# A fused attention and mixture-of-experts kernel: the first expert's row numbers by one-hot products, its second layer and the second expert's tiles as scheduled steps

## The chip, the cores and the metric

The kernel runs on one core of a Trainium2 chip. The metric is the time of one execution on the device in microseconds (us), lower is better. Before the change three runs gave 637.39, 641.42 and 641.85; the median is 641.42. The engines are TensorE (PE in the profile; PEld is its weight load), VectorE (DVE), ScalarE (ACT), GpSimd (POOL) and SyncE (SP), which issues most transfers. Each engine takes its instructions in the order of the program.

## The reference

```python
# q, k, v: (4, 8, 576, 64); first the sum of two attentions
out_d  = softmax(q_d @ k_d.T / 8) @ v_d          # q_d, k_d, v_d: means over 4 neighbouring positions
scores = where(|i - j| < 4, q @ k.T / 8, -1e9)   # local attention at full length
x      = repeat(out_d, 4) + softmax(scores) @ v  # then 2304 rows of 512
# then a mixture of 8 experts, two for each row
lg     = x @ w_gate + log1p(exp(x @ w_noise)) * noise
top2, wts = the two largest of lg, and their softmax
out[rows of e] += wts[:, None] * (relu(x[rows of e] @ w1[e]) @ w2[e])   # w1: 512x1024, w2: 1024x512
```

## The kernel before

**Stages.** The attention output is made in 18 chunks of 128 rows. Of each chunk TensorE makes a transposed copy that is stored as rows of x_d in memory (`l_xt`, line 690), and the router's numbers (`l_lg`, line 707, and their sum `l_ls`, line 716). Chunks are routed in groups: chunks 0 to 3, 4 to 7, 8 to 11, 12 and 13, 14 to 17. Routing a group gives noisy logits, the two best experts, each row's position in its expert's list (sums over rows as products with a triangle, `r_pos`, lines 768 to 771), and two weights. For each chunk two indirect transfers of GpSimd then scatter row number and weight into list_d in memory (`r_put`, line 836): 36 scatters in all.

**Expert 0** has 630 rows, 5 tiles of 126, made in two parts so that it can begin before the last group is routed. Part one is 3 tiles, the rows of the first three groups (`GA` = 2 is the last of them). Its row numbers come back from list_d: once the first 24 scatters are out, SyncE reads the list (`a_list`, 997), VectorE clears the empty places (`a_rows`, 1008), GpSimd gathers the rows of x (`gather0`, 1011), VectorE reorders them (`b_order`, 1106), TensorE transposes them (`b_pe`, 1113), and ScalarE and VectorE cut each tile into a high and a low half (`b_hi`, `b_lo`). Part two, 2 tiles, has its row numbers without memory: for each of the last six chunks VectorE marks, in a 128x256 table, which place of the list a row takes (`r_hot`, 787), and 12 products of these tables with the row numbers give the list (`b_list`, 800). The first layer (`b_gemm`, 1133) goes over 8 chunks of 128 hidden columns; each product with a weight is three products of halves (high by high, high by low, low by high), so 96 products for each part. The second layer (`gemm2`, 1230) is 24 products of 512 columns for each tile; VectorE scales the result (1236), and GpSimd scatters it into the output (1240).

**Experts 1 to 7** are a loop written out by hand. In the second layer of expert e the table `BESIDE` (for e = 0 the table `FIRST`) says after which product block the rows of expert e + 1 are gathered (G), turned in blocks of 32 by VectorE (`turn_xt`, 1169), moved to their places by ScalarE and VectorE (`move_xt`, 1180 and 1182) and cut in halves (H).

**What sets the order.** All up to expert 0's first layer, with the loads of its second layer's weights, is a list of `Step`s: an engine, an assumed duration, what it comes after, and a priority. `run_steps` takes for each engine the step that can begin first and among several the lowest priority, and so writes each engine's order. A table `OFF` adds a number for each kind of step to its priority. Buffers are rings; a step that needs a slot comes after the users of the slot's last owner. Where the planned clock leaves TensorE idle, `keep_warm` fills the gap with products on a tile of ones (line 373); nobody reads them. The order is fixed when the program is built; on the chip each engine waits wherever something is late.

## Time and profile before

| | before |
|---|---|
| median of three runs | 641.42 us |
| lowest, highest | 637.39, 641.85 us |
| the profiled execution, its span and its own time | 644.8 us |
| TensorE busy | 613.5 us, 95% |
| VectorE, ScalarE, GpSimd busy | 412.1, 348.7, 241.6 us |

The profiled execution is one execution recorded by the hardware profiler, 3.4 us above the median. Times in the rows are microseconds from the start of its span. The names in a row (out<-in) are those of the program's tiles: xT is a chunk of attention output, lg and m are the router's logits and choices, xr a tile of gathered rows, ptg its transpose, ph0a and ph0b the first layer of parts one and two, hot a table of marks. "x16" at a row's end counts instructions taken together. A figure in square brackets is the idle time before, with what ended it. The clock column is the share of TensorE's full clock that was granted. Matmul records overlap, since a product's tail runs beside the next product's start.

### The profile page before, as it was taken

The page shows a single profiled execution, that of the slowest core. Times are in us where ns is not written, and L with a number is a line of the kernel's source. Part 1 is how long each engine was busy: PE and PEld are TensorE (multiplying, and loading weights), DVE is VectorE, ACT ScalarE, POOL GpSimd, SP SyncE. Part 2 cuts the span into 40 slices and gives each one's busy share as a digit, 9 for nine tenths or more (in the row PEclk, how much of TensorE's full clock was granted, in tenths as well). Part 3 has the DMA queues.
Part 4 walks back from the last instruction along what each step waited for, and adds up shares of the span by engine and source line. Part 5 has one row for each costly group of instructions (what it writes and reads, how often), then busy time and mean ns, then how long its engine had stood idle before and what let it go on. Part 6 is the DMA issues. An engine that isn't in the chain of part 4 may idle for free. (4 is left out here: it accounts for less than half of the span.)

```text
span 644.8 us, 12872 instructions
## 1 busy us (share of the span) xinstructions
PE 613.5 (95%) x4770; PEld 535.4 (83%) x4770; DVE 412.1 (64%) x1029; ACT 348.7 (54%) x810; POOL 241.6 (37%) x310
## 2 busy tenths in 40 slices
PE   8989998899899999999999999999999999999993
PEld 7768686777798889988987998998899899889982
DVE  5898689688584693874676487467647736753310
ACT  7877487585543573762574376256438616733200
POOL 5574758665444223232322323323132333222111
PEclk9999899899799999999999999999999999999997
DMA  9998985776744344543654454354455436444111
GB/s 157 190 193 188 191 198 142 209 205 163 209 80 109 96 154 144 149 129 116 179 156 142 129 156 134 115 172 145 140 144 147 146 118 167 134 141 125 56 45 34
DMA packets 136760, 92.63 MB, mean 144 GB/s; under 512 B 72028, under 2 KB 118620, under 8 KB 136688
## 3 DMA queue, kind: packets, MB, share of 16 engines
q1 hardware_dynamic: 125136, 62.71, 39.6%
q0 software_dynamic: 11552, 29.01, 15.1%
q8 instruction: 39, 0.64, 0.4%
q14 instruction: 33, 0.27, 0.2%
HBM read 72.62 MB, written 19.95 MB: 144 GB/s over the span
## 5 line engine op out<-in xcount | busy, mean ns | idle before, releaser
L1205 PE MATMUL ph<-xh,w0l 128*128 128x316 f32 x448 | 138.1, 308 | 0.0
L1205 PE MATMUL ph<-xl,w0h 128*128 128x316 f32 x448 | 138.0, 308 | 0.0
L1205 PE MATMUL ph<-xh,w0h 128*128 128x316 f32 x448 | 138.0, 308 | 0.0
L1230 PE MATMUL py<-w1l,hh 128*126 128x512 f32 x320 | 126.2, 394 | 0.0
L1230 PE MATMUL py<-w1h,hh 128*126 128x512 f32 x320 | 126.2, 394 | 0.0
L1230 PE MATMUL py<-w1h,hl 128*126 128x512 f32 x320 | 126.1, 394 | 0.0
L1209 ACT ACTIVATE hh<-ph 128x632 fp32r<-128x632 f32 x56 | 39.1, 699 | 134.9 <-PE ph L1205 134.9
L1240 POOL DMA_INDIRECT out_dram<-ga,lt x40 | 45.0, 1124 | 175.2 <-DVE ga L1239 123.8
L1210 DVE SCALAR_TENSOR_TENSOR hl<-ph,hh 128x632 fp32r<-128x632 f32 x56 | 45.8, 817 | 85.5 <-ACT hh L1209 84.7
L1180 ACT ACTIVATE xr<-tr 32x128 f32<-32x128 f32 x280 | 86.3, 308 | 5.0 <-DVE tr L1169 1.1
L1205 PEld LDWEIGHTS ph<-xl,w0h 128*128 128x128 f32 x448 | 84.3, 188 | 0.3
L1205 PEld LDWEIGHTS ph<-xh,w0h 128*128 128x128 f32 x448 | 84.2, 188 | 0.3
L1205 PEld LDWEIGHTS ph<-xh,w0l 128*128 128x128 f32 x448 | 84.2, 188 | 0.0
L1230 PEld LDWEIGHTS py<-w1l,hh 128*126 128x126 f32 x320 | 59.7, 186 | 14.6
L1230 PEld LDWEIGHTS py<-w1h,hl 128*126 128x126 f32 x320 | 59.6, 186 | 14.4
L1230 PEld LDWEIGHTS py<-w1h,hh 128*126 128x126 f32 x320 | 59.6, 186 | 14.3
L1239 DVE SCALAR_TENSOR_TENSOR ga<-py,lt,ga 126x512 f32<-126x512 f32 x35 | 26.3, 751 | 68.2 <-PE py L1230 68.2
L1218 POOL DMA_INDIRECT ga<-out_dram,cl x35 | 38.1, 1090 | 83.5 <-PE ph L1205 60.9
L1182 DVE COPY xr<-tr 32x128 f32<-32x128 f32 x280 | 64.2, 229 | 3.5
L201 ACT ACTIVATE w0h<-raw 128x512 fp32r<-128x512 f32 x64 | 39.0, 624 | 37.0 <-DMA raw<-in_moe_w_dram 36.9
L1085 POOL DMA_INDIRECT gx<-x_d,cl x35 | 36.5, 1043 | 55.0 <-PE ph L1205 32.5
L836 POOL DMA_INDIRECT list_d<-pay,sli x36 | 36.8, 1022 | 34.3 <-PE pb L800 8.1
(176 smaller groups left out, 1022.8 us busy)
## 6 DMA issues: line engine op xcount, KB each, us to landing
raw<-in_moe_w_dram SPq DMA_DIRECT2D x128, 256.0 KB
vw<-in_v_dram SPq DMA_DIRECT2D x80, 64.0 KB
x_d<-x SPq DMA_DIRECT2D x18, 256.0 KB
out_dram<-zero SPq DMA_DIRECT2D x6, 768.0 KB
nat<-in_q_dram SPq DMA_DIRECT2D x16, 256.0 KB
nat<-in_k_dram SPq DMA_DIRECT2D x16, 256.0 KB
vg<-in_v_dram SPq DMA_DIRECT2D x8, 320.0 KB
vg<-in_v_dram SPq DMA_DIRECT2D x8, 256.0 KB
```

The source lines that it names most:

```text
L201: nc.scalar.activation(hi, raw, AF.Copy)
L836: ins = nc.gpsimd.indirect_dma_start(out=list_d[:, :], out_offset=bass.IndirectOffsetOnAxis(ap=sli[:, kk, i : i + 1], axis=0), in_=pay[:, ...
L1085: ins = nc.gpsimd.indirect_dma_start(out=gx, out_offset=None, in_=x_rows[:, :], in_offset=bass.IndirectOffsetOnAxis(ap=lists[e][1][:, t : ...
L1180: nc.scalar.activation(dst, src, AF.Copy)
L1182: nc.vector.tensor_copy(dst, src)
L1205: last_mm[0] = nc.tensor.matmul(ph[:, n, 0:NH], lhsT=w[:, c, :], rhs=xx[:, c, sl], start=(c == 0 and z == 0), stop=(c == NDC - 1 and z == 2))
L1209: nc.scalar.activation(hh, ph[:, :, 0:NH], AF.Relu)
L1210: nc.vector.scalar_tensor_tensor(out=hl, in0=ph[:, :, 0:NH], scalar=0.0, in1=hh.bitcast(F32), op0=ALU.max, op1=ALU.subtract)
L1218: after_pe(nc.gpsimd.indirect_dma_start(out=acc[:TR], out_offset=None, in_=out[:, :], in_offset=bass.IndirectOffsetOnAxis(ap=cl[:TR, t : t ...
L1230: last_mm[0] = nc.tensor.matmul(py[:TR], lhsT=hx[:, sl], rhs=w, start=(f == 0 and z == 0), stop=(f == NFC - 1 and z == 2))
L1239: nc.vector.scalar_tensor_tensor(out=acc[:TR], in0=py[:TR], scalar=wt, in1=acc[:TR], op0=ALU.mult, op1=ALU.add)
L1240: nc.gpsimd.indirect_dma_start(out=out[:, :], out_offset=bass.IndirectOffsetOnAxis(ap=lt[:TR, t, 0:1], axis=0), in_=acc[:TR], in_offset=No ...
```

## The change

1. *Part one's row numbers.* The first three groups get marks too: for each chunk a table of 128x256 for tiles 0 and 1 and one of half the width for tile 2 (`r_hot`, 24 marks more). For each of these groups 12 products on TensorE (`a_part`) add up to lists, and VectorE adds them over the groups (`a_acc`). The gather of part one comes after the last of these sums, no more after the list in memory. The list is still read, for the weights of part one and for what other chunks put into part two (`a_list`, `a_rows`).
2. *Second layer of expert 0* as steps: four blocks of 6 products for each tile (`o_part`), a scaling (`o_mul`) and a scatter (`o_put`), so tiles of part one can go ahead of part two's first layer.
3. *Expert 1's tiles* as steps, by the way of expert 0: reorder (`e_order`), four transposes on TensorE (`e_pe`), two halves (`e_hi`, `e_lo`), in place of turn and move. Its first-layer weights are steps too (`fetch_e`, `hi_e`, `lo_e`). The table `FIRST` goes, and the written-out loop begins at expert 1.
4. *New priorities* for nearly every kind of step, attention among them.

```diff
@@ -320,21 +320,23 @@
-        "a_count": -34.4, "a_holes": 34.1, "a_list": -12.6, "a_rows": 8.5, "b_gather": -16, "b_gemm": 8,
-        "b_rest": 24.4, "b_rows": -40, "b_weights": 40, "c_count": -49, "c_fills": -30.5, "c_first": 25.6,
...
+        "a_acc": -44.2, "a_count": -60, "a_holes": 6, "a_list": 10.6, "a_part": -60, "a_rows": 25.3,
+        "b_gather": -60, "b_gemm": 30.3, "b_hi": 10.9, "b_list": -11.9, "b_lo": -21.5, "b_order": -10.6,
+        "b_pe": -23.8, "b_relu": -27.6, "b_rest": -44.4, "b_rows": 35.1, "b_weights": -26.1, "c_count": -49,
...
@@ -782,11 +784,42 @@
                                        in1=st["pos", g][:, :ni, 0], op0=ALU.mult, op1=ALU.add)
+        def one(name):
+            return sm.tile([P, 2 * P], BF16, tag="hot", name=name, bufs=sum(ni_ for _, ni_ in groups[GA + 1 :]))
+
+        def mark_(dst, i, base):
+            nc.vector.tensor_scalar(dst, iota_b[:, : dst.shape[1]], far[:, i : i + 1], float(FAR - base), op0=ALU.subtract, op1=ALU.is_equal)
+
         for i in range(ni):
-            hot = sm.tile([P, 2 * P], BF16, tag="hot", name=f"hot{g}_{i}", bufs=sum(ni_ for _, ni_ in groups[GA + 1 :]))
-            nc.vector.tensor_scalar(hot, iota_b, far[:, i : i + 1], float(FAR - NA), op0=ALU.subtract, op1=ALU.is_equal)
-            hots.append((hot, n0 + i))
-
+            hot = one(f"hot{g}_{i}")
+            mark_(hot, i, NA if g > GA else 0)
+            if g > GA:
+                hots.append((hot, n0 + i))
+                continue
+            if i % 2 == 0:
+                two = one(f"hot{g}_{i}s")
+            rest = two[:, P * (i % 2) : P * (i % 2) + P]
+            mark_(rest, i, 2 * TR)
+            hots_a.append(((hot[:, 0:P], hot[:, TR : TR + P], rest), n0 + i))
+
+    def a_part(g):
+        pa = bank(RA, 2 * NTA, f"pa{g}").rearrange("p (t c) -> p t c", c=2)
+        for t in range(NTA):
+            for i, (hot, n) in enumerate(hots_a):
+                nc.tensor.matmul(pa[:, t], lhsT=hot[t], rhs=idp[:, n], start=(i == 0), stop=(i == len(hots_a) - 1))
+        hots_a.clear()
+        st["pa", g] = pa
+
+    def a_acc(g):
+        pa = st.pop(("pa", g))
+        if g == 0:
+            nc.vector.tensor_copy(sum_a, pa)
+        else:
+            nc.vector.tensor_tensor(sum_a, sum_a, pa, op=ALU.add)
+        if g == GA:
+            nc.vector.scalar_tensor_tensor(out=cl0[:, :NTA], in0=sum_a[:, :, 0], scalar=64.0, in1=sum_a[:, :, 1], op0=ALU.mult, op1=ALU.add)
+
+    hots_a = []
     hots = []
@@ -974,6 +1007,7 @@
     cle = xo.tile([P, NT - NTA], F32, tag="cle", name="cle")
+    sum_a = xo.tile([P, NTA, 2], F32, tag="sum_a", name="sum_a")
     scatters_by = {}
@@ -994,7 +1028,7 @@
         src = list_d[t0 * TR : t1 * TR, :]
-        ins = nc.sync.dma_start(out=lt[:TR], in_=src.rearrange("(t p) c -> p t c" if t0 else "(p t) c -> p t c", p=TR))
+        ins = nc.sync.dma_start(out=lt[:TR], in_=src.rearrange("(t p) c -> p t c", p=TR))
         wait_for(ins, scatters)
@@ -1003,9 +1037,8 @@
-        for lt, cl in ((lt0[:, :NTA], cl0[:, :NTA]), (lte, cle)):
-            ids_ = lt[:TR, :, 0]
-            nc.vector.scalar_tensor_tensor(out=cl[:TR], in0=ids_, scalar=float(N), in1=ids_, op0=ALU.is_lt, op1=ALU.mult)
+        ids_ = lte[:TR, :, 0]
+        nc.vector.scalar_tensor_tensor(out=cle[:TR], in0=ids_, scalar=float(N), in1=ids_, op0=ALU.is_lt, op1=ALU.mult)
@@ -1028,7 +1061,11 @@
         b3 = Step("r_where", "dve", 0.11, lambda g=g, n0=n0, ni=ni: r_where(g, n0, ni), after=[b3, s_holes], use=[ppb], **pr_)
-        s_hot = Step("r_hot", "dve", 0.2 + 0.2 * ni, lambda g=g, n0=n0, ni=ni: r_hot(g, n0, ni), after=[b3], light=True, prio=n1 + KH) if g > GA else None
+        s_hot = Step("r_hot", "dve", 0.2 + (0.2 if g > GA else 0.34) * ni, lambda g=g, n0=n0, ni=ni: r_hot(g, n0, ni), after=[b3, s_ids], light=True, prio=n1 + KH)
+        if g <= GA:
+            pab = buf(RA)
+            s_acc = Step("a_part", "pe", 0.07 * ni * NTA, lambda g=g: a_part(g), after=[s_hot], new=[pab], prio=n1 + KH)
+            s_acc = Step("a_acc", "dve", 0.1 if g < GA else 0.25, lambda g=g: a_acc(g), after=[s_acc], use=[pab], prio=n1 + KH)
         b5 = Step("r_slot", "dve", 0.75, lambda g=g, n0=n0, ni=ni: r_slot(g, n0, ni), after=[b3], **pr_)
@@ -1041,8 +1078,8 @@
             s_list = a1 = Step("a_list", "sp", 0.9, a_list, after=list(s_put), light=True, prio=n1 + 2.0, move=0.3)
-            a1 = Step("a_rows", "dve", 0.15, a_rows, after=[a1, s_ids], light=True, prio=n1 + 2.0)
-            s_gxa = [Step("b_gather", "pool", 1.05, lambda t=t, r=(n0 + ni) * P: b_gather(t, r), after=[a1] + s_store[: n0 + ni], light=True, prio=n1 + 2.0, lag=3.2, stage=2)
+            s_rows = Step("a_rows", "dve", 0.15, a_rows, after=[a1, s_ids], light=True, prio=n1 + 2.0)
+            s_gxa = [Step("b_gather", "pool", 1.05, lambda t=t, r=(n0 + ni) * P: b_gather(t, r), after=[s_acc] + s_store[: n0 + ni], light=True, prio=n1 + 2.0, lag=3.2, stage=2)
                      for t in range(NTA)]
@@ -1190,6 +1227,49 @@
         nc.vector.tensor_tensor(xl, xr, xh.bitcast(F32), op=ALU.subtract)
+
+    def w1_again(f, hi):
+        (split_hi if hi else split_lo)(1, 0, f)
+
+    def o_part(t, c):
+
+        if c == 0:
+            st["py", t] = ps_t.tile([P, DM], F32, tag="tp", name=f"py0_{t}")
+        py, sl = st["py", t], slice(t * TR, (t + 1) * TR)
+        for f in range(OC * c, OC * (c + 1)):
+            hh, hl = hts[f]
+            wh, wl = w2s[f]
+            for z, (hx, w) in enumerate(((hh, wh), (hl, wh), (hh, wl))):
+                mark[0] = nc.tensor.matmul(py[:TR], lhsT=hx[:, sl], rhs=w, start=(f == 0 and z == 0),
+                                 stop=(f == NFC - 1 and z == 2))
+
+    def o_mul(t):
+        acc = ga_p.tile([P, DM], F32, tag="ga", name=f"ga0_{t}")
+        nc.vector.tensor_scalar(acc[:TR], st.pop(("py", t))[:TR], lt0[:TR, t, 1:2].bitcast(F32), None, op0=ALU.mult)
+        st["acc", t] = acc
+
+    def o_put(t):
+        nc.gpsimd.indirect_dma_start(
+            out=out[:, :], out_offset=bass.IndirectOffsetOnAxis(ap=lt0[:TR, t, 0:1], axis=0),
+            in_=st.pop(("acc", t))[:TR], in_offset=None, bounds_check=N - 1, oob_is_err=False)
+
+    def e_order(t):
+
+        xr = xe_p[0].tile([P, NDC, 4, 32], F32, tag="xr", name=f"xr1_{t}", bufs=2)
+        nc.vector.tensor_copy(xr.rearrange("p c a i -> p a c i"), gxs.pop((1, t)).rearrange("p (a c i) -> p a c i", a=4, c=NDC))
+        st["xr", t] = xr
+
...
+    OC = 2
...
@@ -1244,14 +1320,16 @@
     xe_p, h_p = [None, None], None
+    s_g, s_h, s_w2 = {}, ([], []), []
+    R.update({"gx": Ring(3), "ga": Ring(6)})
     for part in range(2):
...
             a1 = Step("b_list", "pe", 0.4, b_list, after=[s_hot, s_ids], new=[pbb], light=True, prio=KB)
-            a1 = Step("b_rows", "dve", 0.27, b_rows, after=[a1], use=[pbb], light=True, prio=KB)
-            a2 = Step("b_weights", "sp", 0.45, lambda: list0(lt0[:, NTA:], NTA, NT), after=list(s_put), prio=34, move=0.3, stage=3)
+            a1 = Step("b_rows", "dve", 0.27, b_rows, after=[a1, s_rows], use=[pbb], light=True, prio=KB)
+            a2_w = Step("b_weights", "sp", 0.45, lambda: list0(lt0[:, NTA:], NTA, NT), after=list(s_put), prio=34, move=0.3, stage=3)
         s_x = []
@@ -1265,7 +1343,9 @@
             a2 = Step("b_relu", "act", 0.1 + 1.7 * w_, lambda f=f, part=part: b_relu(f, part), after=[a1_], use=[phb], prio=25, light=True, stage=sg)
-            Step("b_rest", "dve", 0.1 + 2.5 * w_, lambda f=f, part=part: b_rest(f, part), after=[a2], use=[phb], prio=25, light=True, stage=sg)
+            if part:
+                s_g[f] = a1_
+            s_h[part].append(Step("b_rest", "dve", 0.1 + 2.5 * w_, lambda f=f, part=part: b_rest(f, part), after=[a2], use=[phb], prio=25, light=True, stage=sg))
     pb = buf("tp")
@@ -1273,11 +1353,31 @@
         a2 = Step("split_hi2", "act", 0.52, lambda f=f: split_hi(0, 1, f), after=[a1], use=[rb], prio=45 + f, stage=3)
-        Step("split_lo2", "dve", 0.6, lambda f=f: split_lo(0, 1, f), after=[a2], use=[rb], prio=45 + f, stage=3)
+        s_w2.append(Step("split_lo2", "dve", 0.6, lambda f=f: split_lo(0, 1, f), after=[a2], use=[rb], prio=45 + f, stage=3))
+    for t in range(NT):
+        pyb, gab, a1_ = buf("tp"), buf("ga"), None
+        for c in range(NFC // OC):
+            a1_ = Step("o_part", "pe", OC * 3 * 0.232, lambda t=t, c=c: o_part(t, c), cols=OC * 3 * 512,
+                       after=[a1_] + s_h[t >= NTA][OC * c : OC * c + OC] + s_w2[OC * c : OC * c + OC] + ([s_h[1][OC * c + OC - 1]] if t >= NTA else []),
+                       new=[] if c else [pyb], use=[pyb] if c else [], prio=60 + 5 * t + c, stage=3)
+        a1_ = Step("o_mul", "dve", 0.65, lambda t=t: o_mul(t), after=[a1_, a2_w if t >= NTA else s_list], use=[pyb], new=[gab], prio=60 + 5 * t, stage=3)
+        Step("o_put", "pool", 1.25, lambda t=t: o_put(t), after=[a1_], use=[gab], prio=60 + 5 * t, lag=3.0, stage=3)
     a1 = Step("load_list", "sp", 0.9, lambda: load_list(1), after=list(s_put), prio=33, move=0.3, stage=3)
     a1 = Step("list_rows", "dve", 1.0, lambda: list_rows(1), after=[a1], prio=33, stage=3)
-    for t in range(3):
-        a1 = Step("gather", "pool", 1.3, lambda t=t: gather(1, t), after=[a1], prio=50 + t, lag=2.0, stage=3)
+    s_e = []
+    for t in range(NT):
+        gxb, xrb, ptb = buf("gx"), buf("xr"), buf("tp")
+        a2 = Step("gather", "pool", 1.05, lambda t=t: gather(1, t), after=[a1], new=[gxb], prio=50 + t, lag=4.0, stage=3)
+        a3 = Step("e_order", "dve", 0.35, lambda t=t: e_order(t), after=[a2], use=[gxb], new=[xrb], prio=KB + 45 + t, stage=3)
+        a4 = Step("e_pe", "pe", 0.43, lambda t=t: b_pe(t), cols=512, after=[a3], use=[xrb], new=[ptb], prio=KB + 45 + t, stage=3)
+        a5 = Step("e_hi", "act", 0.48, lambda t=t: e_hi(t), after=[a4], use=[ptb], prio=KB + 45 + t, stage=3)
+        s_e.append(Step("e_lo", "dve", 0.6, lambda t=t: e_lo(t), after=[a5], use=[ptb], prio=KB + 45 + t, stage=3))
+    for f in range(NFC):
+        rb = buf("raw")
+        a1 = Step("fetch_e", "sp", 0.45, lambda f=f: fetch_w(1, 0, f), new=[rb], prio=70 + f, move=1.2, stage=3)
+        a2 = Step("hi_e", "act", 0.52, lambda f=f: w1_again(f, True), after=[a1, s_g[f]], use=[rb], prio=70 + f, stage=3)
+        s_e.append(Step("lo_e", "dve", 0.6, lambda f=f: w1_again(f, False), after=[a2], use=[rb], prio=70 + f, stage=3))
+    Step("e_go", "pe", 0.01, lambda: None, after=s_e[: NT + 2], prio=200, stage=3)
     run_steps(1)
@@ -1301,22 +1401,22 @@
               8: "M2 N2 H1 G3", 9: "T3 H2 G4", 10: "M3 N3 T4", 11: "M4 N4 H3", 12: "H4"}
-    FIRST = {8: "T0 T1 G3 M0 N0 H0", 9: "M1 N1 T2 G4 H1", 10: "M2 N2 T3 H2", 11: "M3 N3 T4 H3", 12: "M4 N4 H4"}
     def beside(e, slot):
-        for o in (FIRST if e == 0 else BESIDE).get(slot, "").split():
+        for o in BESIDE.get(slot, "").split():
             if o[0] == "A":
...
-    for e in range(E):
+    xeT.pop(0)
+    for e in range(1, E):
         nxt = e + 1 < E
-        if nxt and e > 0:
+        if nxt:
             load_list(e + 1)
             list_rows(e + 1)
-        for f in range(NFC) if e > 0 else ():
+        for f in range(NFC):
             if f == 0:
```

The planner's new numbers and steps change the order on every engine. Here are three places of it; "x16" counts equal rows taken together, and a line of "..." marks rows left out.

TensorE from the last attention product step on (o is attention's output, ones the filler), before:

```order
L659 MATMUL o_119<-pT_3045,vw_2878 64x58 x16
...
L373 MATMUL o_118<-ones 128x128
L690 MATMUL ptx_3176<-ident,xT_3022 128x128 x4
L707 MATMUL pl_3181<-xT_3022,wgn 32x128 x4
...
L716 MATMUL ps_3210<-sel,lgT_3186 128x16
...
L1113 MATMUL ptg_3242<-ident,xr_0_3214 128x128 x4
...
L771 MATMUL pp_3347<-m_3302,tri 128x8
...
L1133 MATMUL ph0a_3433<-xh_2897,w0h_1155 128x378
```

and after:

```order
L661 MATMUL o_119<-pT_2941,vw_2859 64x58 x16
L1150 MATMUL ptg_3112<-ident,xr_2_3109 128x128 x4
...
L375 MATMUL o_118<-ones 128x128
L709 MATMUL pl_3131<-xT_2996,wgn 32x128 x4
L692 MATMUL ptx_3140<-ident,xT_2996 128x128 x4
...
L718 MATMUL ps_3156<-sel,lgT_3136 128x16
L1170 MATMUL ph0a_3164<-xh_2691,w0h_2041 128x378
...
L773 MATMUL pp_3289<-m_3258,tri 128x8
```

The transposes of two of part one's tiles now stand before the last attention step, the third right behind it. The first expert product follows the last chunk's router sum, and the last group's position products (pp) come four chunks of 12 expert products later. Of fillers 9 are left between the attention step and the first expert product, before there were 127.

TensorE at part two's transposes, before:

```order
L1133 MATMUL ph0a_3548<-xh_2897,w0l_2604 128x378
L1113 MATMUL ptg_3580<-ident,xr_3_3577 128x128 x4
L1133 MATMUL ph0a_3592<-xh_2897,w0h_2689 128x378
...
L1113 MATMUL ptg_3623<-ident,xr_4_3617 128x128 x4
...
L1230 MATMUL py_0_3868<-w1h_3395,hh_0_3479 126x512
```

and after:

```order
L1170 MATMUL ph0a_3463<-xh_2691,w0l_3276 128x378
L1243 MATMUL py_0_3491<-w1h_3357,hh_0_3208 126x512
...
L1243 MATMUL py_1_3525<-w1l_3376,hh_1_3243 126x512
L1150 MATMUL ptg_3547<-ident,xr_3_3535 128x128 x4
L1243 MATMUL py_0_3491<-w1h_3517,hh_4_3391 126x512
...
L1150 MATMUL ptg_3571<-ident,xr_4_3552 128x128 x4
```

Second-layer products of tiles 0 and 1 (py) now stand before the transposes of tiles 3 and 4, behind the eight chunks of part one's first layer.

GpSimd between part one's gathers and part two's, before:

```order
L1011 DMA gx_2_3148<-x_d,cl_121 128x512
L835 MEMSET dummy 128x1
L836 DMA list_d<-pay,sli_3137 19456x2
...
L836 DMA list_d<-pay,sli_3463 19456x2
L1011 DMA gx_3_3508<-x_d,cl_121 128x512
```

and after:

```order
L1044 DMA gx_2_2967<-x_d,cl_121 128x512
L868 MEMSET dummy 128x1
L869 DMA list_d<-pay,sli_2857 19456x2
...
L869 DMA list_d<-pay,sli_3398 19456x2
L1044 DMA gx_3_3480<-x_d,cl_121 128x512
```

Five scatters of the list stood between them, now twelve do: seven of the third group, which were ahead of part one's gathers, and five of the last two groups.

## Rows read from the trace of the kernel before

**Rows 1.** Stretches: length, busy us of PE, PEld, DVE, ACT, POOL, clock, DMA, GB/s.
```profile
0.00:165.76 165.76, 150.43 (x2054) 118.96 (x2055) 131.68 (x363) 118.47 (x288) 102.30 (x171) 0.98 0.87 183
165.76:183.06 17.30, 14.40 (x201) 13.00 (x200) 10.53 (x52) 10.05 (x17) 7.65 (x12) 0.80 0.65 169
183.06:215.00 31.94, 29.86 (x216) 28.89 (x214) 18.04 (x50) 10.58 (x22) 14.92 (x20) 1.00 0.43 108
215.00:242.90 27.90, 27.90 (x123) 22.44 (x122) 24.31 (x63) 20.05 (x54) 6.66 (x6) 1.00 0.42 132
242.90:633.80 390.90, 390.90 (x2186) 352.11 (x2184) 226.75 (x502) 189.57 (x430) 109.09 (x100) 1.00 0.45 133
```

**Rows 2.** The same view for line 373 alone, the fillers.
```profile
0.00:165.76 165.76, 20.05 (x260) 17.67 (x260) 0.98 0.87 183
165.76:183.06 17.30, 9.97 (x127) 9.09 (x127) 0.80 0.65 169
```

**Rows 3.** TensorE's own waits: who waited for whom, total us, times, longest.
```profile
PE pp L771 <- DVE m L755: 3.0, 1, 3.0
PE ptx L690 <- DVE xT L681: 2.4, 2, 2.0
```

**Rows 4.** Timeline of TensorE in the handover; start, length, what, idle before.
```profile
165.76 1.14 PE L659 MATMUL o<-pT,vw 64*64 64x58 f32 x32
...
171.12 1.12 PE L690 MATMUL ptx<-ident,xT 128*128 128x128 f32 x4 [1.96 <-DVE xT L681]
172.17 0.65 PE L707 MATMUL pl<-xT,wgn 128*32 128x128 f32 x8
...
173.79 0.55 PE L716 MATMUL ps<-sel,lgT 128*128 128x16 f32 x2
...
177.46 0.61 PE L1113 MATMUL ptg<-ident,xr 128*128 128x128 f32 x4
177.91 0.44 PE L373 MATMUL o<-ones 128*128 128x128 bf16 x5
...
178.63 2.34 PE L373 MATMUL o<-ones 128*128 128x128 bf16 x39
...
183.06 0.42 PE L1133 MATMUL ph0a<-xh,w0h 128*128 128x378 f32 x1
```

**Rows 5.** Stretches of 5 us after two gaps of TensorE, columns as above.
```profile
115.00:120.00 5.00, 5.00 (x84) 4.31 (x84) 3.34 (x18) 1.56 (x3) 0.29 (x1) 0.66 0.93 248
...
170.00:175.00 5.00, 3.88 (x33) 3.17 (x34) 3.42 (x13) 1.27 (x4) 2.28 (x4) 0.54 0.57 182
```

**Rows 6.** Timeline of VectorE and GpSimd in the routing of group 1.
```profile
107.78 2.84 DVE L735 TENSOR_TENSOR sp<-sp,noise_sb 128x32 f32<-128x32 f32 x1 [0.43 <-issue]
...
108.29 1.06 POOL L638 TENSOR_TENSOR sb<-sb,rz 128x512 f32<-128x512 f32 x1
...
109.29 1.27 POOL L487 TENSOR_TENSOR vh<-vg 64x512 f32<-64x512 f32 x1
...
110.66 0.19 DVE L736 TENSOR_TENSOR nl<-sp,lg 128x32 f32<-128x32 f32 x1
...
113.48 1.19 DVE L755 TENSOR_TENSOR m<-oh 128x32 bf16<-128x32 f32 x1
```

**Rows 7.** Timeline of GpSimd: last scatter ahead of part one, first gather.
```profile
158.19 0.97 POOL L836 DMA_INDIRECT list_d<-pay,sli  x1 [0.19 <-issue]
...
166.20 1.00 POOL L1011 DMA_INDIRECT gx<-x_d,cl  x1 [7.04 <-DVE lg L722]
```

**Rows 8.** Timeline of all engines: gather of part two, its reordering copy.
```profile
187.11 1.39 POOL L1011 DMA_INDIRECT gx<-x_d,cl  x1 [0.30 <-DVE cnt L823]
...
192.15 0.49 DVE L1106 COPY xr<-gx 128x512 f32<-128x512 f32 x1 [0.86 <-DMA gx<-x_d,cl]
```

**Rows 9.** Groups by line and shape: marks on VectorE, one-hot products on TensorE.
```profile
L787 DVE TENSOR_SCALAR hot<-iota_b,far 128x256 bf16<-128x256 bf16 x6 | 1.4, 283 | 0.1
...
L800 PE MATMUL pb<-idp,hot 128*128 128x2 bf16 x12 | 0.5, 165 | 0.0
```

43 lines of the change are left out of this document (24 added, 19 removed).

## The prediction

> **What bounds the kernel now.** I read the stretches first, then what TensorE did in them, then its waits. The stretches [rows 1] are cut where the work changes: attention and routing up to the last attention product step (165.76), the handover from there to the first expert product (183.06), the first layer of expert 0 (to 215.0), its second layer (to 242.9), and experts 1 to 7 (to 633.8). From 215.0 on TensorE is busy without a gap: 27.90 of 27.90 us, then 390.90 of 390.90. Only fewer or quicker products help there. Its 120 products of 512 columns in 27.90 us come one each 0.2325 us; by width a product of 378 columns takes 0.172 and one of 256 columns 0.116 (estimates from that row). All that can be won lies ahead of 215. There TensorE idles 15.3 us before 165.76, 2.9 us in the handover and 2.1 us after it, and part of its busy time is filler, products on a tile of ones that nobody reads: 260 of them, 20.05 us, before 165.76 and 127, 9.97 us, in the handover [rows 2]. So filler and idle time are 35 us before 165.76, and 12.9 of the handover's 17.3 us. The longest named waits of TensorE are for VectorE [rows 3].
>
> **What the handover waits for.** Part one's row numbers come through memory: the last scatter ends at 159.16, the gather starts at 166.20 [rows 7], 7.0 us for the list's way out and back. But the transposes of those rows stand between 176 and 179 [rows 4], and a gather needs 5.0 us from issue to the reordering copy (187.11 to 192.15) [rows 8]. So the list's round trip alone is not the limit. The order is: TensorE's queue has the last group's routing (router products, softmax, positions) ahead of the first expert product, and fills the wait, 39 fillers in one piece [rows 4].
>
> **The change, part by part.**
>
> *Handover, +11.8 us.* In the new order only these stand between the last attention step and the first expert product: that step (1.14), one set of four transposes (0.61), 9 fillers, and three small steps of the last chunk (transpose, router product, its sum). Those three took 1.12 + 0.65 + 0.55 = 2.3 us at a granted clock of 0.54 [rows 4, 5], so 1.2 at full clock. A filler is 60 ns at most (39 in 2.34 us with their tail), so 9 are 0.5. That makes 3.4 us, plus the wait for VectorE's addition that makes the last chunk: none at best, 4.3 us as now (166.9 to 171.12) at worst; I take 2.1, the middle, since neither end has a row of the new order. 17.3 - 5.5 = 11.8, bounds 9.6 and 13.9. Position sums and the routing softmax move behind four expert chunks, 48 products or 8.3 us, against 7 us from 173.8 to 181 now, so they are covered; if that cover is short, the position sum is what comes late.
>
> *Before the handover, -1.0 us.* The new order has 149 fillers there, 111 fewer, at 60 to 77 ns (20.05 us / 260) 6.7 to 8.5 us; I take the middle, 7.6. Added on TensorE: three times 12 one-hot products at 0.5 a dozen [rows 9], 1.5 us, and two sets of transposes moved ahead, 0.9 (a set holds TensorE 0.45, from 177.46 to the next filler [rows 4]). Added on VectorE: 12 marks as now (0.283), 12 of half the width (0.14 to 0.283, I take 0.21), seven small steps at the 0.19 of a 128x32 one [rows 6, 9], less one saved: 7.0 us. That is what they cost undisturbed; the six marks of today run where GpSimd only issues transfers. The new ones stand amid attention, where GpSimd computes: it is busy 102.30 of 165.76 us [rows 1]. What that can do is seen at 107.78 [rows 6]: a 128x32 product of VectorE that takes 0.19 us elsewhere took 2.84, over exactly two sums of GpSimd, and another took 1.19, so 3.65 us were lost in one block of routing, and TensorE waited 3.0 us for its end [rows 3] and came back at clock 0.66 [rows 5]. Three blocks of marks lose 0 to 11.0 us in this way; I take half, 5.5. Of the 12.5 us, I put half on the path, 6.2, as VectorE is busy 79% here, but only 3.4 of TensorE's 15.3 idle us go by name to its two longest waits for it (3.0, and the 0.4 of 2.4 that are not in the handover) [rows 1, 3]. 7.6 - 1.5 - 0.9 - 6.2 = -1.0; bounds +6.1 (marks all hidden) and -13.7 (18 us all on the path).
> The Trainium skill, SBUF — State Buffer, Who interferes with whom, has a rule that speaks against these marks: a VectorE copy, cast or scalar operation may take the port pair that GpSimd uses, and whichever starts first keeps it for its whole instruction. The trace agrees as far as the 2.84 us go, though VectorE's instruction there had two inputs, which the section names as a case of its own. By the rule each of the 24 marks can be caught, which is the third rival below; if none were, the sum would be 6.2 us lower.
>
> *Scatters.* GpSimd now has 12 scatters between part one's and part two's gathers, 5 before, each 0.97 us of issue [rows 7], 12 to 16 us with what lies between. TensorE has 72 expert products (12.4), a last attention step and small ones in that time, and the second gather waits for the one-hot list after them anyway, so the scatters do not hold it up. Behind that list stand 24 + 18 products, 4.1 + 4.2 us, against the 5.0 of the gather [rows 8] and some VectorE steps: tight, at most 1 us late. On SyncE the list read for part one's weights now waits for 24 scatters with all eight second-layer loads queued behind it; they are due after the first layer's 96 products of part one, 16.5 us.
>
> *First layer, +0.7 us.* 2.1 us of idle time there; second-layer products now stand around part two's transposes. I take 1.0 of it (0 to 2.1), less 0.3 for the positions moved in.
>
> *Second layer and expert 1, -2.2 us.* The same 120 products. Five sets of transposes join TensorE, 0.45 each: -2.2. VectorE and ScalarE lose 80 small copies, worth nothing, because TensorE had no gap there. The rows of expert 1 need the list after all 36 scatters, of which the last now waits behind the first output tile on GpSimd. Chain: the result's step, taken as 1, two issues 2.0, list 7.0, five issues and a landing 10 [rows 7, 8], in all 20 us. Cover: 96 products of 256 columns and 84 of 512, 30.7 us. Hidden with 11 us to spare; without them it would stand on the path.
>
> Experts 1 to 7 are unchanged: 0. **Sum: 11.8 - 1.0 + 0.7 - 2.2 = 9.3 us faster.** The profiled execution spans 644.8 us, so 635.5; it lies 3.4 above the median of the runs, 641.42, and the same step from there gives **632.1 us**.
>
> **Rivals.** One per cent, about what a measurement can tell, is 6.4 us: 635.0 and 647.8.
> *The fillers bought nothing* (0.18). If the waits they covered stay, idle time takes their place before 165.76: 7.6 us less, 639.7. For it: the longest named waits are VectorE's [rows 3]. Against it: much of TensorE's queue is merely placed otherwise, and 111 fillers could go only since other work was ready in the plan.
> *The marks are not caught* (0.13). No collision and all 7 us hidden: 6.2 more, 625.9. For it: VectorE has 34 us free ahead of 165.76. Against it: the 2.84 us.
> *VectorE's marks hold up attention* (0.09), the slower side. Each of 24 marks waits for a GpSimd sum of some 1.06 us [rows 6], 25 us, with the 7.0 us all on the path: 11.8 + 7.6 - 2.4 - 32 + 0.7 - 2.2 = -16.5, or 658. It makes the kernel slower by 1% from 0.6 us of waiting a mark on. Against it: in the second half of attention GpSimd mostly issues scatters, beside which the present marks ran in 0.283.
> The clock is no rival of its own: each of the two rows in [rows 5] cost some 2 us, and the one at 170 goes with its gap.
>
> **How the numbers follow.** The forecast has 0.60, its own range 624 to 640 by the bounds of handover and marks. Some 0.10 of it lies within 1%. So faster 0.60 - 0.10 + 0.13 + 0.02 = 0.65, within 1% 0.10 + 0.16 = 0.26, slower 0.09. The range of 623 to 641 leaves out the slower rival and the best tail.
>
> **What would show it.** Right: the first expert product near 172 instead of 183 with under 1.5 us of filler ahead of it after the last attention step; the last attention step at 162 to 170; second-layer products without gaps, expert 1 starting near 234. Marks: 24 at 0.2 to 0.3 us, or some of 1 us and more beside GpSimd's sums. Wrong: idle time before the last attention step over 25 us; a gap of more than 2 us between the one-hot list and part two's transposes; TensorE waiting for expert 1's rows.

## The result and the profile after

The changed kernel took 633.44 us (median of four runs, 631.28 to 638.53) against 640.69 for the kernel before: 7.3 us less by the medians. The ratio is 0.990, interval 0.9856 to 0.9944, or 6.4 us less (3.6 to 9.2). On another chip, in the first experiment, the ratio was 0.9862 (0.9824 to 0.990), 8.9 us. Forecast were 9.3 us and 632.1. All ratios below, and differences in us worked out from them, are to runs of the kernel before on the same chip, whose median lay between 641.5 and 647.5.

The profiled execution after spans 633.0 us. The same view by stretches as [rows 1], cut at the last attention step, the first expert product, expert 1's first product and the end of the last expert's products; then line 375, the fillers, as in [rows 2]:

```profile
0.00:163.99 163.99, 148.92 (x1987) 117.84 (x1987) 130.63 (x403) 119.25 (x289) 100.14 (x166) 0.95 0.89 191
163.99:167.33 3.34, 3.34 (x60) 2.86 (x60) 2.88 (x8) 2.18 (x6) 1.53 (x4) 1.00 0.34 100
167.33:231.86 64.53, 61.13 (x370) 53.73 (x370) 37.74 (x107) 24.42 (x47) 28.44 (x40) 1.00 0.51 135
231.86:622.20 390.34, 390.34 (x2185) 351.50 (x2183) 226.66 (x501) 189.74 (x430) 108.60 (x100) 1.00 0.44 133
```

```profile
0.00:163.99 163.99, 13.81 (x149) 11.52 (x149) 0.95 0.89 191
163.99:167.33 3.34, 0.83 (x9) 0.67 (x9) 1.00 0.34 100
```

The handover shrank from 17.30 us to 3.34, with TensorE busy all through it and its clock at 1.00 instead of 0.80. Attention got 1.8 us shorter. Expert 0 got longer: 64.5 us, where 183.06 to 242.9 were 59.8 [rows 1]. TensorE idles 3.4 us of it, 2.1 before; the rest is work that joined the stage, five sets of transposes above all. Experts 1 to 7 are the same within 0.6 us. TensorE's timeline of the handover, where [rows 4] stood, shows no wait at all:

```profile
163.99 1.14 PE L661 MATMUL o<-pT,vw 64*64 64x58 f32 x32
165.07 0.66 PE L1150 MATMUL ptg<-ident,xr 128*128 128x128 f32 x4
165.56 0.55 PE L375 MATMUL o<-ones 128*128 128x128 bf16 x7
166.04 0.43 PE L709 MATMUL pl<-xT,wgn 128*32 128x128 f32 x8
166.40 0.66 PE L692 MATMUL ptx<-ident,xT 128*128 128x128 f32 x4
166.89 0.28 PE L375 MATMUL o<-ones 128*128 128x128 bf16 x2
167.09 0.40 PE L718 MATMUL ps<-sel,lgT 128*128 128x16 f32 x2
167.33 0.42 PE L1170 MATMUL ph0a<-xh,w0h 128*128 128x378 f32 x1
```

Behind it there are waits that [rows 3] did not have. TensorE's own waits (total, times, longest), of which the first falls before the handover and the others in the stage of expert 0:

```profile
PE o L661 <- DMA vw<-in_v_dram: 2.7, 3, 1.2
...
PE py L1243 <- ACT w1h L201: 1.4, 1, 1.4
...
PE pc L1192 <- DVE cnt L856: 1.3, 1, 1.3
...
PE ptg L1150 <- DVE xr L1143: 0.7, 1, 0.7
```

One profiled execution is not exact to a microsecond. The changed kernel's second profile, on the other chip, has these three starts at 166.40, 169.83 and 237.76 and spans 639.1: attention 2.4 us longer, expert 0 67.9 us. The profile of before is of the first chip only and lay 3.4 us above its median; on the chip of the second profile the kernel before took 6 us more by its median, so that profile has no true partner. The handover's gain of 12 to 14 us is sure (15.3 us is the shortest handover of any kernel with the list); a difference of 2 or 3 us in another stretch is not, unless runs bear it out.

### The profile page after: what moved, and what is told of

Read it like the earlier page. It is cut to its first block, busy times and chain, and to the rows that moved or that the text cites. A ratio compares the mean times of both kernels' runs of the same rounds, so it can differ in the third digit from the quotient of the medians.

```text
span 633.0 us, 12482 instructions
## 1 busy us (share of the span) xinstructions
PE 603.8 (95%) x4598; PEld 525.9 (83%) x4598; DVE 398.7 (63%) x1019; ACT 335.6 (53%) x770; POOL 239.7 (38%) x310
## 4 chain that ended last, share of the span: by engine, by line
PE 82%; DMA 7%; ACT 3%; POOL 3%; DVE 2%; issue 1%; SPq 1%; POOLq 0%; DVEq 0%
PE ph L1285 31%; PE py L1310 31%; PE py L1243 3%; PE o L661 3%; DMA raw<-in_moe_w_dram 2%; PE ph0b L1170 2%; PE sc L613 2%; PE pt L438 2%; DMA vw<-in_v_dram 2%; PE ptx L692 1%; PE od L576 1%; PE ptl L646 1%; DMA vg<-in_v_dram 1%; POOL list_d L869 1%; PE ptd L554 1%
## 5 line engine op out<-in xcount | busy, mean ns | idle before, releaser
L1310 PE MATMUL py<-w1h,hl 128*126 128x512 f32 x280 | 110.4, 394 | 0.0
L1310 PE MATMUL py<-w1h,hh 128*126 128x512 f32 x280 | 110.3, 394 | 0.0
L1310 PE MATMUL py<-w1l,hh 128*126 128x512 f32 x280 | 110.3, 394 | 0.0
L1316 POOL DMA_INDIRECT out_dram<-ga,lt x35 | 39.2, 1120 | 155.0 <-DVE ga L1315 123.7
L1217 ACT ACTIVATE xr<-tr 32x128 f32<-32x128 f32 x240 | 74.0, 308 | 3.4
L1310 PEld LDWEIGHTS py<-w1l,hh 128*126 128x126 f32 x280 | 52.1, 186 | 12.9
L1310 PEld LDWEIGHTS py<-w1h,hh 128*126 128x126 f32 x280 | 52.2, 186 | 12.6
L1310 PEld LDWEIGHTS py<-w1h,hl 128*126 128x126 f32 x280 | 52.1, 186 | 12.5
L1219 DVE COPY xr<-tr 32x128 f32<-32x128 f32 x240 | 54.6, 227 | 3.0
```

Of the source, the lines that this page charges most:

```text
L1217: nc.scalar.activation(dst, src, AF.Copy)
L1219: nc.vector.tensor_copy(dst, src)
L1310: last_mm[0] = nc.tensor.matmul(py[:TR], lhsT=hx[:, sl], rhs=w, start=(f == 0 and z == 0), stop=(f == NFC - 1 and z == 2))
L1316: nc.gpsimd.indirect_dma_start(out=out[:, :], out_offset=bass.IndirectOffsetOnAxis(ap=lt[:TR, t, 0:1], axis=0), in_=acc[:TR], in_offset=No ...
```

## The experiments

The start of the last attention step, of the first expert product and of expert 1, the two stretches between them, and the ratio to before. Each row of starts is one profiled execution. The first two are of one chip, one-hot sums alone and steps alone of a third, the others of the chip called the other:

| kernel | last step | first product | expert 1 | handover | expert 0 | ratio (interval) |
|---|---|---|---|---|---|---|
| before | 165.8 | 183.1 | 243.0 | 17.3 | 59.9 | 1 |
| changed | 164.0 | 167.3 | 231.9 | 3.3 | 64.5 | 0.990 (0.986 to 0.994) |
| changed, other chip | 166.4 | 169.8 | 237.8 | 3.4 | 67.9 | 0.986 (0.982 to 0.990) |
| new priorities alone | 162.1 | 190.9 | 248.8 | 28.8 | 58.0 | 1.009 (1.005 to 1.013) |
| one-hot sums alone | 175.8 | 177.4 | 250.9 | 1.6 | 73.5 | 1.016 (1.011 to 1.021) |
| steps alone | 168.8 | 184.1 | 245.9 | 15.3 | 61.8 | 1.005 (1.002 to 1.008) |
| changed, old priorities | 176.6 | 178.2 | 243.0 | 1.6 | 64.7 | 1.001 (0.998 to 1.005) |
| changed, without the steps | 168.4 | 171.8 | 243.7 | 3.4 | 71.9 | 0.997 (0.994 to 1.000) |

**The yardstick, and parts undone.** The changed kernel again:

> The changed kernel once more, beside the next three on one chip, as their yardstick. Its profiled execution was 11.8 us shorter than that of before (span 633.0 against 644.8), its runs 7.3 us by their medians (633.4 against 640.7). If the profiled execution of before lay high, the difference here is 6 to 9 us; if the profiles are the truer pair, 11 to 13.

It measured 8.9 us, within the first range (10.1 by the medians, between the two), so the profile of before most likely had lain high. Then the old code with the new numbers, which undoes one-hot sums and steps at once:

```diff
     OFF = {
-        ... (the old number of every kind)
+        ... (the new number of every kind that the old code has)
```

> The kernel before, its code unchanged, with the new priorities for the kinds of steps it has. Theory A (the gain needs the one-hot sums, since they free the first expert product from the list in memory): no gain; the planner leaves 224 fillers between the last attention step and the first expert product, against 127 before, so the handover stays at 17 us or grows to 22, while some 2 us are saved ahead of it: 639 to 645. Theory B (the gain is the reordering by new priorities, whatever the code): 632 to 635.

Slower by 6.0 us (0.9 %): no gain, as theory A had it, but more than the 4 us that its range allowed. Attention ended 3.7 us earlier, and the handover grew to 28.8 us, of which 16.8 are fillers; the stretch and its fillers:

```profile
162.06:190.86 28.80, 22.59 (x335) 21.00 (x331) 14.98 (x80) 11.85 (x22) 15.16 (x23) 0.82 0.54 139
```

```profile
162.06:190.86 28.80, 16.82 (x224) 15.27 (x224) 0.82 0.54 139
```

So the new numbers alone gain nothing: with the list in memory the earlier end of attention only lengthens the wait behind it. The last group's position products were over at 174.8 there, and still the first expert product came at 190.9, behind the transposes of part one's rows, the last of them at 187.4. Those rows' gathers began at 173.5. What ended last there was the rows that come by the list, and not the last group's routing. Next, the new code with the old numbers (the same edit the other way round):

> The changed code with the old priorities for the kinds of steps that existed before (new kinds keep theirs). Theory A: the handover is short all the same (10 fillers in the plan), 3 to 6 us instead of 17; ahead of it the plan holds about as many fillers as before, so the 2 us gained there go: 634 to 637. Theory B: 640 or more.

No change (0.1 % slower), where theory A wanted 634 to 637 at a level of 641, some 1 % less. Its half on the handover held, and more, 1.6 us. But the last attention step came at 176.6, 11 us late: the stretch ahead of it, and TensorE's products at the third group's marks with the idle time before each:

```profile
0.00:176.63 176.63, 153.16 (x2055) 119.78 (x2055) 141.78 (x408) 122.86 (x294) 106.56 (x175) 0.96 0.87 182
```

```profile
149.39 0.18 PE L809 MATMUL pa<-idp,hot 128*128 128x2 bf16 x1 [0.58 <-DVE hot L791]
149.75 0.18 PE L809 MATMUL pa<-idp,hot 128*128 128x2 bf16 x1 [0.18 <-DVE hot L791]
150.11 0.18 PE L809 MATMUL pa<-idp,hot 128*128 128x2 bf16 x1 [0.18 <-DVE hot L791]
...
152.35 3.57 PE L554 MATMUL ptd<-ident,pd 128*80 128x128 f32 x16 [1.51 <-DVE pd L547]
```

In a stretch that is 10.9 us longer VectorE is 10.1 us busier than in [rows 1], and TensorE idles 23.5 us instead of 15.3. The one-hot products stand in TensorE's queue just behind the marks, so that TensorE takes them one mark at a time, and attention's own product pd, behind eight marks (149.05 to 150.58) in VectorE's queue, is late after them. In the changed kernel those products come after the marks are done, at 149.04, without a wait. Named waits for marks are only 1.9 us here; which others make up the rest was not taken apart.

Next, the second layer and expert 1's tiles written out as before:

```diff
-    for t in range(NT):
-        pyb, gab, a1_ = buf("tp"), buf("ga"), None
...
+    FIRST = {8: "T0 T1 G3 M0 N0 H0", 9: "M1 N1 T2 G4 H1", ...
-    for e in range(1, E):
+    for e in range(E):
```

> The changed kernel with the second layer of expert 0 and the tiles of expert 1 written out as in the kernel before; one-hot sums and new priorities stay. The stage of expert 0 lasted 64.5 us in the changed kernel and 59.8 before. Theory C (the steps cost time: five sets of transposes 2.0, a wait of 1.8 for the second layer's weights, 1.3 for a count): 2 to 4 us faster than the changed kernel. Rival D (the early second-layer products fill the wait for part two's rows, which would come back without them): 0 to 3 us slower than the changed kernel.

Theory C was wrong. Without the steps the gain is 1.9 us, 7.1 less than that of the changed kernel on the same chip: rival D had the direction, and less than half of the size. Expert 0 takes 71.9 us. Its stretch, the fillers in it, TensorE's timeline from the end of part one's first layer, and VectorE's at the second tile:

```profile
171.83:243.69 71.86, 67.35 (x450) 60.74 (x450) 47.18 (x146) 36.30 (x87) 28.90 (x40) 0.95 0.45 119
```

```profile
171.83:243.69 71.86, 7.71 (x101) 7.13 (x101) 0.95 0.45 119
```

```profile
192.80 3.92 PE L375 MATMUL pw<-ones 128*128 128x128 bf16 x63
197.08 0.66 PE L1150 MATMUL ptg<-ident,xr 128*128 128x128 f32 x4 [0.36 <-DVE xr L1143]
...
200.83 0.71 PE L1150 MATMUL ptg<-ident,xr 128*128 128x128 f32 x4 [2.49 <-DVE w1l L206]
```

```profile
199.64 0.69 DVE L206 TENSOR_TENSOR w1l<-raw,w1h 128x512 fp32r<-128x512 f32 x1 [2.62 <-ACT w1h L201]
200.25 0.44 DVE L1143 COPY xr<-gx 128x512 f32<-128x512 f32 x1
```

Part two's rows do not come earlier because part one begins earlier: the transposes stood at 192.70 (behind the copy at 192.15 [rows 8]) and 197.00 before, at 191.44 and 193.32 in the changed kernel, here at 197.08 and 200.83. In the eight profiles of the table the first of them stands 3 to 26 us behind the first expert product, but always 24.5 to 32.0 us behind the start of the last attention step, and the last group can be routed only after that step. Part one's first layer is over at 186.4 in the changed kernel and at 192.8 here, and then come fillers and idle time until the rows are there. The steps put second-layer products in that place.

Not all of that wait is the rows' own. Their gathers were issued at 189.94 and 191.24, and the reordering copies began at 196.60 and 200.25, 6.7 and 9.0 us later, where [rows 8] has 5.0. In VectorE's queue cuts of second-layer weights stand ahead of the copies, and the last of them waited 2.62 us for its high half. How the 7.1 us divide between the missing products and this order was not tested.

The fourth way to pair the parts, steps and new priorities with the list kept, was not run. That the handover needs the one-hot sums rests on all kernels together: nine with them have 1.6 to 6.8 us there, four with the list 15.3 to 28.8.

**The other two corners.** One-hot sums alone, and steps alone, each with the old priorities:

> The kernel before with the one-hot sums alone: old priorities, second layer and expert 1's tiles written out as before. Theory C (without the early second-layer products the wait for part two's rows returns, as in the run without the steps, where the stage of expert 0 took 71.9 us against 64.5, and the old priorities let the marks delay attention, as in the run with old priorities, where the last attention step began at 176.6 instead of 165.8): 5 to 8 us slower than the kernel before. Rival (the steps are worth nothing by themselves): within 2 us of the kernel before, as the run with old priorities was.

> The kernel before with the steps alone: second layer of expert 0 and tiles of expert 1 as steps, row numbers of part one through the list, old priorities. Theory C: the first layer of part one ends after part two's rows are there, so early second-layer products have no wait to fill, and five more sets of transposes stand on TensorE: 0 to 3 us slower than before. Rival (the steps save time by themselves, as forecast, 2.2 less): 2 us faster.

One-hot sums alone are 10.2 us slower, more than expected, with both losses in the table: attention to 175.8 and expert 0 at 73.5 us. Steps alone are 2.9 us slower, at the upper end of what theory C allowed: without an early first layer there is no wait for them to fill, and expert 0 takes 1.9 us longer. In its profile attention also ends 3.0 us later, for which no cause was sought. So three edits that are worth +10.2, +2.9 and +6.0 us one by one, and +0.6 and -1.9 in the two pairs that were run, are worth -6 to -9 together.

**The price of the marks.** Each of the 24 new marks made twice:

```diff
             mark_(rest, i, 2 * TR)
+            mark_(hot, i, 0)
+            mark_(rest, i, 2 * TR)
```

> The changed kernel with each of the 24 new marks made twice (the same values into the same tile, planner's durations unchanged): 6.3 us more work for VectorE amid attention, at 0.28 and 0.25 us a mark. If the marks are hidden: 0 to 1.5 us slower than the changed kernel. If half of their time stands on the path, as forecast: 3 us slower. If all of it, or if they meet GpSimd's sums often: 6 us and more.

The ratio is 0.9875 (0.9825 to 0.9924), 0.13 % or 0.8 us above that of the changed kernel on the other chip. That is the value for hidden marks, but with these intervals the forecast's 3 us are not shut out. In the one profile attention hid them only in part: VectorE spent 10.0 us more on marks, not 6.3, since more of them met GpSimd; TensorE waited 3.6 us for marks, and the last attention step began at 169.8, 5.8 and 3.4 us later than in the changed kernel's two profiles. Expert 1 began at 236.0, between those two, so the stages behind gave it back in that execution. In the changed kernel some marks meet GpSimd too. Here are the timelines of VectorE and GpSimd at the second group's marks in the changed kernel, as in [rows 6], and its marks by shape:

```profile
104.52 0.24 DVE L791 TENSOR_SCALAR hot_0s<-iota_b,far 128x128 bf16<-128x128 bf16 x1
...
104.98 1.04 POOL L640 TENSOR_TENSOR sb<-sb,rz 128x512 f32<-128x512 f32 x1
105.03 1.08 DVE L791 TENSOR_SCALAR hot_2s<-iota_b,far 128x128 bf16<-128x128 bf16 x1
```

```profile
L791 DVE TENSOR_SCALAR hot<-iota_b,far 128x256 bf16<-128x256 bf16 x18 | 5.9, 349 | 0.2
...
L791 DVE TENSOR_SCALAR hot_2s<-iota_b,far 128x128 bf16<-128x128 bf16 x6 | 2.3, 385 | 0.0
L791 DVE TENSOR_SCALAR hot_0s<-iota_b,far 128x128 bf16<-128x128 bf16 x6 | 1.5, 247 | 0.0
```

The mark at 105.03 takes 1.08 us instead of 0.25 and ends when GpSimd's product does. That is one mark in 24, and five more took 0.42 to 0.65; undisturbed, at 0.28 and 0.25, the 24 would take 6.4 us, and they took 8.0 (5.9 less six marks of part two at 0.28, and 3.8).

**What the fillers do.** The changed kernel, and the one before, without the fillers behind the plan's first 8 us:

```diff
     def keep_warm(t, t1):
+        if t1 > 8.0:
+            return max(t, t1)
```

> The changed kernel without the fillers after the first 8 us of the plan: 137 of 168 fillers go, some 12 us of TensorE's time. Theory F (fillers stand in waits and keep the clock up): their time turns into idle time, the clock ahead of the first expert product falls below the 0.95 of the changed kernel, and the kernel is 3 to 15 us slower than it. Rival (fillers stand on the path): 3 to 12 us faster than the changed kernel.

> The kernel before without the fillers after the first 8 us of the plan: 356 of 387 go, some 27 us of TensorE's time, 10 of them in the handover. Theory F (fillers stand in waits and keep the clock up): idle time in their place, a lower clock, 5 to 25 us slower than before. Rival (fillers stand on the path): 5 to 20 us faster, and then fewer fillers were what the changed kernel gained by.

Ratios 0.9947 (0.9916 to 0.9978), 3 to 5 us slower than the changed kernel by its two ratios (the interval of one of them overlaps), and 1.0041 (1.0012 to 1.0069), 2.6 us slower than before, less than either theory had it. Both theories were half right. Fillers do stand on attention's path: without them its last step comes at 157.9 and 155.7, 6 to 10 us earlier, and in the changed kernel the clock ahead of it stays at 0.95, against theory F. It is given back behind it. The handover stretch of both kernels, and the first expert product of the second:

```profile
157.91:164.68 6.77, 5.04 (x78) 4.23 (x78) 4.66 (x18) 5.06 (x10) 4.50 (x9) 1.00 0.58 181
```

```profile
155.65:177.62 21.97, 8.62 (x103) 6.11 (x103) 15.26 (x82) 10.76 (x20) 12.05 (x19) 0.65 0.63 155
```

```profile
177.62 0.68 PE L1135 MATMUL ph0a<-xh,w0h 128*128 128x378 f32 x1 [0.68 <-ACT xh L1120]
```

The kernel before then idles 13.4 of 22.0 us, the clock is at 0.65, and the first product takes 0.68 us instead of 0.42. In the changed kernel without fillers expert 0 takes 68.5 us, of which TensorE idles 5.4. Part two's second set of transposes stands at 200.1 there, although its rows were in order at 189.9: ahead of it in TensorE's queue are second-layer products, which waited 0.9 us twice for their weights, and behind it 1.8 us went on waiting for the tile's low half. So fewer fillers were not in themselves what the change gained by.

**Which priorities.** New ones for attention's steps alone, in the changed code:

> The changed code with new priorities for the steps of attention alone; routing, transfers of weights and expert 0 keep the old ones. With all priorities old, the last attention step began at 176.6; with all new, at 164.0 and 166.4. If the order of attention's own steps is what hides the marks: at 164 to 168, and the time within 4 us of the changed kernel. If it is the place of the routing steps (which sums TensorE and VectorE meet first): 173 or later, and within 3 us of the kernel before.

Slower by 8.5 us (0.9 to 1.8 %), with the last attention step at 177.6. Attention's own numbers by themselves do not hide the marks; the outcome fits the rival's place for the cause and not its time, as it is worse than either theory's range. The numbers work as a set, and no subset was found to explain them.

**The new waits.** The count's product was put later, and the planner given a truer cost for the weights:

```diff
-        "c_count": -49,
+        "c_count": 30,
-        a1 = Step("fetch_w2", ..., prio=31 + f, move=1.0, stage=3)
+        a1 = Step("fetch_w2", ..., prio=31 + f, move=1.8, stage=3)
```

> The changed kernel with the product that adds up all counts, which nothing waits for until the end, put behind the first layer of part two by its priority, and with 1.8 instead of 1.0 us a piece in the planner's costs for the second layer's weights (eight took 16.2 us in the profile, and TensorE waited 1.4 and 2.0 us for one). TensorE idled 1.3 and 1.6 us ahead of the count, and its clock was lower behind both waits in the second profile. If these waits end last there: 3 to 5 us faster than the changed kernel. If the next one takes their place (part two's rows, the last weights): no difference, and the stage of expert 0 stays at 64 to 68 us.

0.9819 (0.9775 to 0.9863), 11.7 us faster than before, the fastest ratio of all; against the changed kernel's two ratios 3 to 5 us, with intervals that overlap. Its one profile has expert 0 at 65.7 us, between the changed kernel's two, and a wait of 2.0 us at part two's transposes in place of that at the count, while 0.8 us of waiting for a weight is left. That it beats the changed kernel is not shown. On top of it, the zeroing transfers were spread:

```diff
     def l_store(n):
+        stored.append(n)
+        for k in {11: (3,), 12: (4,)}.get(len(stored), ()):
+            fill_out(k)
...
+        if n == 19:
+            fill_out(5)
```

> The kernel of the run with the late count, with three transfers that zero half of the output (768 KB each) no longer in one piece ahead of the values of the last attention steps: one goes ahead of the eleventh stored chunk, one ahead of the twelfth, one behind the last values. In the changed kernel SyncE issued them from 137.7 to 142.2, the next values took until 148.4 to issue, TensorE waited 1.9 us for values at 155 and 156, and its clock there was 0.56 and then 0.76. If that piece of transfers is the cause: 2 to 5 us faster than the run with the late count, 14 to 17 faster than before, the last attention step at 160 to 163. If another wait is right behind: no difference.

Attention's last step came at 161.1, as expected. The time did not: 6.6 us faster than before, where 14 to 17 were forecast. The same 5 us, in the changed kernel and then in this one:

```profile
155.00:160.00 5.00, 3.98 (x45) 3.36 (x46) 1.77 (x11) 0.53 (x2) 2.19 (x4) 0.56 1.00 279
```

```profile
155.00:160.00 5.00, 3.58 (x52) 2.80 (x44) 2.80 (x14) 4.13 (x8) 4.45 (x7) 1.00 1.08 337
```

TensorE's clock there is 1.00 instead of 0.56. Its waits for values went from 2.7 us to 1.9 in all, the longest from 1.2 to 0.8. Its ratio, 0.9897 (0.9859 to 0.9935), is not better than without the spreading, although its profiled execution, 629.5 us, is the shortest of all. On different chips these two could not be told apart, and whether the spreading gains anything stays open.

## Why the prediction came out as it did

*Handover.* Right, and a little more: 14.0 us against 11.8 with an upper bound of 13.9. The term set too high was the wait for the last chunk's addition, 2.1 us taken and none found. The reason given is less sure. The prediction said that the list's round trip was not the limit and the order was; but every kernel with one-hot sums has 1.6 to 6.8 us there, and every kernel with the list 15 to 29, with new numbers and a new order too. No run moved the last group's routing behind the first expert product and kept the list, so the two are not separated.

*Before the handover.* Forecast -1.0, measured +1.8 and -0.6 in the two profiles. Its parts were off in both directions. Fillers fell by 6.2 us (7.6 forecast), though the experiment without fillers shows that such time is not simply won. VectorE's added work was set at 12.5 us with its collisions, half of it on the path; the marks took 8.0, of which collisions were 1.6 and not 5.5. What ate the fillers' gain was TensorE's other work: 135.1 us (148.92 less 13.81) against 130.4, of which 2.4 are the one-hot products and transposes counted on. The rest fits a clock of 0.95 instead of 0.98, lost at waits like the one at 155; no run isolates it. The prediction also left out what the new priorities do to VectorE: the routing product of 2.84 us in [rows 6] has no like there (0.47 at most), and VectorE is no busier ahead of the handover (130.6 us) than before (131.7), in spite of the marks. In the old code with the new numbers it is busy 125.3 us. Its sentence on the rule of the ports, that without collisions the sum would be 6.2 us lower, doesn't follow from its own terms: half of 5.5 is 2.8, and 6.2 takes the marks themselves as hidden too.

*The stage of expert 0.* This is the step that failed. Its two terms together were set at 1.5 us of loss, and it lost 4.6 in the first profile and 8.0 in the second, which has no partner of before on its chip. In the first, idle time makes most of the miss: 3.4 us where 1.1 were left by the forecast. There are three waits, in the rows above, and two of them the prediction does not have. The second-layer weights, costed at nothing since they were "due after the first layer's 96 products of part one", were waited for 1.4 and 2.0 us; the planner's early second-layer products want them sooner, and the eight loads took 16.2 us. The count's product waited 1.3 and 1.6 us. For part two's rows "at most 1 us late" held by the letter, 0.7 us, but only because the count had held TensorE up before; with the count put later this wait was 2.0. The chain from the one-hot list to the transposes took 10.6 us, where 8.3 were covered. Its gather took 5.9 us to the reordering copy (184.96 to 190.81); "some VectorE steps" ahead of it were more. The list's products ended at 180.83, and VectorE took up their sums only at 184.00, behind 12 other steps:

```profile
180.84 0.55 DVE L1184 SCALAR_TENSOR_TENSOR hl<-ph0a,hh 128x378 fp32r<-128x378 f32 x1
...
183.92 0.17 DVE L1200 TENSOR_SCALAR cnt_i<-cnt_i 128x9 int32<-128x9 int32 x1
184.00 0.15 DVE L838 TENSOR_TENSOR cle<-cle,pb 128x2 f32<-128x2 f32 x1
184.18 0.16 DVE L839 SCALAR_TENSOR_TENSOR cl<-pb,cle 128x2 int32<-128x2 f32 x1
184.96 0.99 POOL L1044 DMA_INDIRECT gx<-x_d,cl  x1 [0.30 <-DVE w1l L206]
```

The new priorities are the likely cause: that of `b_rows`, the step at 184.00, went from -40 to 35.1. The sums lay for 1.8 to 5.7 us in all eight profiles with the new number, and for at most 0.5 in five of the six with the old one (2.7 in the kernel before without fillers). No run changed this one number alone.

In the second profile the clock fell behind the waits at count and weights: 0.66 in 185 to 190 and 0.75 in 200 to 205.

```profile
185.00:190.00 5.00, 4.93 (x20) 4.92 (x20) 3.33 (x14) 0.49 (x1) 3.42 (x6) 0.66 0.44 53
...
200.00:205.00 5.00, 3.00 (x12) 2.20 (x11) 2.05 (x3) 1.11 (x2) 0.91 (x1) 0.75 0.59 142
```

More important, the early second-layer products were named for a microsecond of idle time. They are what turns the earlier start into time: with the steps written out 4 to 7 us of the handover's 14 go back into waits for part two's rows (71.9 us against 64.5 and 67.9). The sum was right although this link was not seen.

*The rivals.* Fillers bought something, but not in the way either side had it. The marks were hardly caught, 1.6 us in 24, near to the rival that gave 625.9; that its time did not come lies in the stage of expert 0 and in TensorE's other work ahead of the handover. The slower rival did not happen in this kernel; its mechanism, marks that hold up attention, has a part in what happens to the same code with the old priorities, whose attention ends 11 us late and not 32.

Of the signs named beforehand, the first expert product (167.3), its fillers (0.83 us) and the last attention step (164.0) came, the first even earlier than said; second-layer products without gaps did not. The total, 9.3 against 7.3 and 8.9, is thus right by a handover worth 2 more and a stage of expert 0 worth 3 to 6 less than forecast. That these two offset each other is luck.

## What to carry to other kernels

When a wait is taken out, find what comes next in the same chain that does not move: here part two's rows, which hang on the last group's routing and stood 24.5 to 32 us behind the last attention step wherever part one began. The time is won only if independent work can be put into the wait that then grows, and that work has inputs (here weights) that must come sooner too. And where priorities are set for a whole plan, test edit and numbers together: each alone was slower, by 3 to 10 us. Then look for single steps that the new numbers put far back in a queue, as here the two short VectorE steps ahead of a gather.

## What the runs showed of the hardware

A VectorE instruction with one bf16 tensor input, 0.25 us alone, took 1.08 beside a GpSimd product of 1.04 and ended with it (105.03). With each mark made twice, one of 0.28 took 2.00. So what [rows 6] showed for products of two inputs happens to marks too. It cost 1.6 us in 24 marks here, and 5.3 in the 48 of the other run. The second case, timelines of VectorE and GpSimd:

```profile
111.79 1.02 POOL L871 DMA_INDIRECT list_d<-pay,sli  x1 [0.24 <-DVE hot L791]
...
112.21 2.00 DVE L791 TENSOR_SCALAR hot<-iota_b,far 128x256 bf16<-128x256 bf16 x1
...
112.83 1.28 POOL L489 TENSOR_TENSOR vh<-vg 64x512 f32<-64x512 f32 x1
```

The mark is recorded as starting 0.62 us before GpSimd's product, and still it ends with it (114.21 and 114.11). The Trainium skill, SBUF — State Buffer, Who interferes with whom, lets whichever starts first keep the ports for its whole instruction. By the recorded starts this pair does not agree. But a scatter of GpSimd is recorded across the mark's start, from 111.79 to 112.81 (the marks at 111.85 and 112.05 took 0.28 and 0.29 us beside it), and GpSimd's spans are rough, so the order of the grants itself was not seen.
